# Off-by-one attention with soft expert mixing: two wide products for the negated maxima, and weight pieces fetched in halves

## The chip, the cores and the metric

The kernel runs on one core of a Trainium2 chip. The metric is the device time of one execution in microseconds (us). The core's engines are TensorE (PE, with its weight loads shown apart as PEld), VectorE (DVE), ScalarE (ACT), GpSimd (POOL) and SyncE (SP); DMA transfers are issued from queues of SP and POOL.

## What is computed

Attention over 8 batches and 12 heads, with 448 positions of 64 elements; its softmax has an extra term in the denominator. The result, as 3584 rows of 768, goes through a soft mixture of 8 experts with 4 slots each.

```python
# attention
scores = scale * np.matmul(q, k.transpose(0, 1, 3, 2))
m = np.max(scores, axis=-1, keepdims=True)
e = np.exp(scores - m)
attn = e / (np.sum(e, axis=-1, keepdims=True) + np.exp(-m) + 1e-09)
x = np.matmul(attn, v)            # then laid out as [3584, 768]
# mixture
logits = x @ phi                  # [3584, 32]
d = softmax of logits over the rows; slot_input = d.T @ x
slot_out = relu(slot_input[e] @ w1[e]) @ w2[e]      # for each expert e
out = (softmax of logits over the slots) @ slot_out
```

## The kernel before

**Units and steps.** The attention is done in 24 units (`U`). A unit is two batches (index `b`) times two heads (index `h`): unit `u` is batch pair `u // 6` and head pair `u % 6`. A unit has 7 steps (`TB = 7`), each for 64 of the 448 positions.

A step of the main loop (lines 751 to 761) issues, in this order:

- `stage_S(u, s)`: scores of 128 query rows against all keys. For steps 0 to 5 these are two products with 64 rows and 128 columns of the array, one for each head (L242); for step 6 they are four products of 64 by 64 (L246). VectorE takes the row maxima of the result (L250).
- work planned as "av" and "value": `stage_AV` (L322), the product of the exponentials and the values of an earlier unit, 12 products of 64 by 128 and then 4 of 64 by 64 for each of the 7 position blocks; in step 5 also the transposes of a finished unit (`stage_X`, L402) and of the next unit's q and k (`stage_T`, L227); in step 0 `stage_MT` of the unit before.
- `stage_ST`, ten steps behind `stage_S` (`LAG = 10`): the scores again, transposed, with the negated maxima added, into one PSUM slot, and ScalarE's exponential of them (L295).
- work planned as "end" and "load": parts of the mixture, and DMA issues.

**The negated maxima.** `stage_MT` transposes the maxima of a unit with four products (L258) into `mt`, a tile of 128 partitions and 64 columns. Each partition holds one row of maxima, for a certain head, batch and position block. GpSimd multiplies `mt` by `nmask`, which is -1 where a partition belongs to a position block and batch and 0 elsewhere, and so spreads it over `md`: 128 partitions by two batches by 448 columns (L268 for the 768 columns of the first six position blocks of both batches, L274 for the 128 of the last block). In `stage_ST` four products with a stationary tile of ones, one for each batch and head (L286), sum the 64 partitions of a head, which gives every output partition the negated maximum of its column. Four more products (L291) add the scores. All eight are 64 by 64 pieces of the array, and all have 448 columns.

**PSUM.** `slot` hands out tiles from a ring of three. A step takes one slot for `stage_S` and one for `stage_ST`; transposes and mixture parts take slots of the same ring.

**Weights.** The experts' weights are fetched in 32 pieces of 128 partitions by 3072 elements (768 KB in the source). 24 of them are resident (`wres`). `load_w` (L156 to L169) issues one DMA on POOL's queue for a piece. The plan (L734) issues one whole piece in step 5 of units 2 to 22, and a second one in units 9, 13 and 16. There it stands behind `load_qk`, which issues the four loads of q and k for the unit after the next and waits until the transposes have read the buffer that it fills.

**What sets the order.** It is written out by hand: `at(n, where, f)` puts a piece of work into step `n`, and each engine runs its instructions in the order in which the loop issues them. `stage_ST` for step `n` follows the "av" and "value" work of the step on TensorE.

**Buffers.** Most tiles lie in one large tile `block` whose parts are listed in L73 to L77 (`md0`, `md1` for the spread maxima, with pads that keep other parts at their places).

Of the kernel before, what the change touches and what calls it, by code (L numbers as in the profile page):

```python
# [9 lines left out]
F32 = mybir.dt.float32  # L10
BF16 = mybir.dt.bfloat16
AX = mybir.AxisListType
AF = mybir.ActivationFunctionType
ALU = mybir.AluOpType
PSUM = bass.MemoryType.PSUM

P = 64
# [3 lines left out]
WRES = 24  # L21
# [3 lines left out]
def kernel(  # L25
# [10 lines left out]
    nc = tc.nc  # L36

    B, H, S, D = q.shape
# [5 lines left out]
    TB = S // P  # L44
# [4 lines left out]
    U = BP * HP  # L49
    C3 = TB // 2  # L50
    N2 = 2 * S
# [4 lines left out]
    gdma = nc.gpsimd.dma_start  # L56

    const = ctx.enter_context(tc.tile_pool(name="const", bufs=1))
    small = ctx.enter_context(tc.tile_pool(name="small", bufs=2))
# [8 lines left out]
    def part(name, n, bufs=1):  # L68
        nonlocal size
        parts[name] = size, n, bufs  # L70
        size += n * bufs

    for name, n in (("vr", 2 * N2), ("qk0", 2 * N2), ("qr", N2), ("kr", N2), ("x0", N2),  # L73
                    ("qk1", 2 * N2), ("md0", N2), ("pad0", 256),
                    ("v65", 2 * TB * 66), ("xu", 4 * TB * 65), ("pad1", 328),
                    ("qk2", 2 * N2), ("md1", N2), ("v66", 2 * TB * 66)):
        part(name, n)  # L77
    part("et", N2, 4)
    part("x", N2, HP)
# [10 lines left out]
    def buf(name, i):  # L90
        o, n, bufs = parts[name]
        return block[:, ds(o + (i % bufs) * n, n)]
# [19 lines left out]
    def room(i):  # L112

        return wres[:, i, :] if i < WRES else block[:, ds(rooms[i - WRES], HW)]

    def slot(shape, dtype=F32):
        return ring.tile(shape, dtype, tag="r", name="ps")
# [11 lines left out]
    def load_qk(u):  # L129

        for src, name in ((q, "qr"), (k, "kr")):
            RAW[u, name] = load(u, buf(name, 0).rearrange("p (h n) -> p h n", h=2), src, nc.gpsimd)
# [13 lines left out]
    def load_v(u):  # L146
        t_ = block[:, ds(parts["vr" if u < U - 1 else "qr"][0], 2 * N2)].bitcast(F32).rearrange("p (h n) -> p h n", h=2)
        RAW[u, "vr"] = load(u, t_, v, nc.sync if u else nc.gpsimd)
# [4 lines left out]
    weights = [(kind, 4 * g + e, half) for kind in (1, 2) for g in range(G)  # L153
               for half in range(2) for e in range(4)]

    def load_w(i):  # L156


        kind, e, half = weights[i]
        if kind == 1:  # L160
            J, n = KC // 2, F
            src = moe_w1[e].rearrange("(p j) f -> p j f", p=128)[:, ds(half * J, J), :]
        else:
            J, n = FK // 2, DD
            src = moe_w2[e, ds(half * 128 * J, 128 * J)].rearrange("(p j) f -> p j f", p=128)
        t_ = room(i).rearrange("p (j n) -> p j n", n=n)
        gdma(out=t_, in_=src)  # L167
        for j in range(J):
            W[kind, e, half * J + j] = t_[:, j, :]  # L169

# [3 lines left out]
    ident32 = const.tile([128, 128], F32, name="ident32")  # L174
# [2 lines left out]
    nc.vector.tensor_copy(ident, ident32)  # L177
    first_cast()
    load_qk(1)
    ones = const.tile([128, P], BF16, name="ones")  # L180
    nc.vector.memset(ones, 1.0)

    nmask = const.tile([128, TB, 2], BF16, name="nmask")
    nc.vector.memset(nmask, 0.0)
    for base in (0, -P):
        nc.gpsimd.affine_select(
            out=nmask, in_=nmask, compare_op=ALU.not_equal, fill=-1.0,
            base=base, pattern=[[-1, TB], [-32, 2]], channel_multiplier=1)
    load_v(0)
    M = [const.tile([128, 160], BF16, name=f"m{i}") for i in range(2)]  # L190
    for i in range(2):
# [27 lines left out]
    QT, KT, MD, ET, EM, AV, XU, X, DEN = {}, {}, {}, {}, {}, {}, {}, {}, {}  # L219

    def stage_T(u, name):

        ps = slot([128, 2, S], BF16)
        r = RAW.pop((u, name))
        for t in range(TB):
            for h in range(2):
                nc.tensor.transpose(ps[ds(h * D, D), :, ds(t * P, P)],  # L227
                                    r[:, h, ds(t * D, D)], ident)
        t_ = buf(f"qk{u % 3}", 0)[:, ts(int(name == "kr"), N2)].rearrange("p (b n) -> p b n", b=2)
        nc.vector.tensor_copy(t_, ps)  # L230
        (QT if name == "qr" else KT)[u] = t_

    def maxima(u):
        return M[u % 2][:, ds(32, 128)].rearrange("p (h r) -> p h r", h=2)
# [17 lines left out]
    def stage_MT(u):  # L252

        own = u == 0 or u == U - 1
        ps = slot([128, 2, 32]) if own else AV[u - 1][:, :, ds((2 * C3 + 1) * 65, 32)]
        for half in range(2):
            for a in range(2):
                nc.tensor.matmul(ps[:, a, :], M[u % 2][:, ds(32 - 32 * half, 128)],  # L258
                                 ident[:, ds(half * P + a * 32, 32)], start=(own and half + a == 0),
                                 stop=(half == 1), skip_group_check=True)  # L260
        mt = small.tile([128, P], BF16, tag="mt", name="mt", bufs=1)
        (nc.scalar.copy if u < U - 1 else nc.vector.tensor_copy)(  # L262
            mt.rearrange("p (a n) -> p a n", a=2), ps)
        em = small.tile([128, 2, TB], F32, tag="em", name="em", bufs=3)
        nc.scalar.activation(em, maxima(u)[:, :, ds(0, TB)], AF.Exp, scale=-scale)
        EM[u] = em
        md = buf(f"md{u % 2}", 0).rearrange("p (b n) -> p b n", b=2)
        nc.gpsimd.tensor_tensor(  # L268
            md[:, :, ds(0, C3 * 128)].rearrange("p b (e n) -> p b e n", n=P),
            mt.unsqueeze(1).unsqueeze(1).broadcast_to([128, 2, 2 * C3, P]),  # L270
            nmask[:, ds(0, 2 * C3), :].rearrange("p (b c) a -> p b (c a)", b=2).unsqueeze(3)
                 .broadcast_to([128, 2, 2 * C3, P]),
            op=ALU.mult)
        nc.gpsimd.tensor_tensor(  # L274
            md[:, :, ds(C3 * 128, P)], mt.unsqueeze(1).broadcast_to([128, 2, P]),
            nmask[:, 2 * C3, :].unsqueeze(2).broadcast_to([128, 2, P]), op=ALU.mult)
        MD[u] = md
        if u < U - 1:
            nc.gpsimd.tensor_scalar(em, em, 1e-9, None, op0=ALU.add)

    def stage_ST(u, t):
        ps = slot([128, 2, 512])
        for b in range(2):
            for h in range(2):
                hs = ds(h * D, D)
                nc.tensor.matmul(ps[ds(b * P, P), h, ds(0, S)], ones[hs, :], MD[u][hs, b, :],  # L286
                                 start=True, stop=False)
        for b in range(2):
            for h in range(2):
                hs = ds(h * D, D)  # L290
                nc.tensor.matmul(ps[ds(b * P, P), h, ds(0, S)],  # L291
                                 KT[u][hs, b, ds(t * P, P)], QT[u][hs, b, :],
                                 start=False, stop=True)
        et = buf("et", u * TB + t).rearrange("p (h n) -> p h n", h=2)
        nc.scalar.activation(et, ps[:, :, ds(0, S)], AF.Exp, scale=scale)  # L295
        ET[u, t] = et
# [118 lines left out]
    def mixture(bp, n, at):  # L415
# [119 lines left out]
        if final:  # L535
# [13 lines left out]
            at(n + 5, "small", slot_sum)  # L549
            at(n + 7, "end", slot_in)  # L550
            at(n + 7, "end", lambda: [load_w(WRES + i) for i in (6, 7)])
            at(n + 7, "end", experts_in)
            at(n + 7, "end", experts_hidden)
# [149 lines left out]
    def at(n, where, f):  # L703
        plan.setdefault((n, where), []).append(f)

    for u in range(U):
        n = u * TB
# [23 lines left out]
    for bp in range(BP):  # L731
        mixture(bp, (bp * HP + HP - 1) * TB + 27, at)

    for i, u in enumerate(sorted((*range(2, U - 1), 9, 13, 16))):  # L734
        at(u * TB + 5, "load", lambda i=i: load_w(i))
    at(4, "load", late_constants)
    stage_T(0, "qr")
    stage_T(0, "kr")

    end = TB * U  # L740
    for n, i in ((end - 5, 0), (end - 1, 1), (end + 3, 2), (end + 7, 3), (end + 12, 4),
                 (end + 12, 5)):
        at(n, "load", lambda i=i: load_w(WRES + i))
# [7 lines left out]
    for n in range(last + 1):  # L751
        run(n, "small")
        if n < TB * U:
            stage_S(*divmod(n, TB))
            run(n, "av")
            run(n, "value")
        if 0 <= n - LAG < TB * U:
            stage_ST(*divmod(n - LAG, TB))
        run(n, "value")
        run(n, "end")  # L760
        run(n, "load")
# [56 lines left out]
    for i in range(2, BP * TB):  # L818
# [4 lines left out]
        c, a = divmod(t, 2)  # L823
        cs = ds(32 * c, 32)
        ps = slot([128, 2, 512])
        for half in range(2):
            if i < FT:
                nc.tensor.matmul(ps[:, half, ds(0, 384)], wide[:, ts(i, 128)], so[:, half, :],
                                 start=True, stop=True)
            else:  # L830
                nc.tensor.matmul(ps[:, half, ds(0, 384)], cT[cs, bp, ts(a, 128)], sr[cs, half, :],  # L831
                                 start=True, stop=True, tile_position=(32 * c, 0))
# [34 lines left out]
```

## Time and profile before

| what | value |
|---|---|
| time, median of 3 runs (lowest to highest) | 328.78 us (325.86 to 331.56) |
| the profiled execution: time, and span of its trace | 328.26 us, 326.5 us |
| TensorE clock granted, mean over the span | 0.953 |
| weight pieces kept in `wres` | 24 issues, 768 KB each, 9.3 us to landing (median) |
| loads of q and k, issued from POOL | 46 and 46 issues, 112 KB each, 4.5 and 5.0 us to landing |
| GpSimd's idle time before the q loads, until L227 has read the buffer | 32.0 us |
| GpSimd's second product of the maxima (L274) | 24 times, 399 ns each |
| VectorE's row maxima (L250) | 168 times, 1088 ns each |
| ScalarE's exponentials (L295) | 168 times, 917 ns each |

How to read it: busy times of an engine are the union of its instructions, so two products that run side by side count once. Products are pipelined, and their ends are modelled: a product of 448 columns is shown with some 360 ns, of which its columns take only a part, so the start of the next product says more than the end of the last. "Issue" is time in which an engine waited for nothing that the profile shows. Operations are named by line and by the tiles that they write and read; an operation that the program puts into `block` is shown under that name.

### The profile page before, as it was taken

What the parts mean: (1) busy time and instruction counts of PE and PEld (TensorE: products, weight loads), DVE (VectorE), ACT (ScalarE), POOL (GpSimd) and SP (SyncE); (2) the same over time, 40 slices, a digit from 0 to 9 for tenths busy, and PEclk for the clock granted to TensorE, in tenths of its full rate; (3) what the DMA queues carried; (4) which work ended last, traced back from release to release, by engine and by line L of the source; (5) the groups of instructions that cost most, each with busy time, mean ns of one, the idle gap of its engine ahead of it and who ended that gap; (6) DMA issues with size and microseconds to landing.
All of it is one profiled execution on the core that took longest, in us unless ns stands there. A gap on an engine that the chain in (4) does not pass through costs nothing.

```text
span 326.5 us, 13241 instructions
## 1 busy us (share of the span) xinstructions
PE 281.1 (86%) x5866; PEld 159.0 (49%) x5866; DVE 253.5 (78%) x354; ACT 211.5 (65%) x341; POOL 207.3 (64%) x308
## 2 busy tenths in 40 slices
PE   0669999999999999998999998989999897977910
PEld 0325565555655556554555555555555453532300
DVE  1897999999989989998899888888998547216820
ACT  3015878878778677786787876867877873215610
POOL 5365678898877887888849866969695653300000
PEclk9999999999999999999999999999999999997555
DMA  7346599999998899999998999988799599947997
GB/s 137 66 60 112 102 175 180 178 176 175 179 186 158 131 210 211 194 178 180 216 189 129 165 228 208 153 154 171 167 134 199 103 189 214 214 95 272 398 400 284
DMA packets 30313, 59.33 MB, mean 182 GB/s; under 512 B 4048, under 2 KB 22736, under 8 KB 30256
## 3 DMA queue, kind: packets, MB, share of 16 engines
q0 software_dynamic: 19056, 36.46, 65.2%
q1 hardware_dynamic: 11200, 22.02, 21.0%
q8 instruction: 46, 0.75, 0.9%
q14 instruction: 11, 0.09, 0.1%
HBM read 83.46 MB, written 11.01 MB: 289 GB/s over the span
## 4 chain that ended last, share of the span: by engine, by line
PE 55%; DVE 19%; POOL 6%; DMA 6%; issue 5%; ACT 4%; SPq 0%; POOLq 0%; ACTq 0%; DVEq 0%
PE av L322 13%; DVE m L250 11%; PE ps L242 9%; PE ps L286 9%; PE ps L291 7%; PE ps L227 5%; DMA block<-in_moe_w_dram 4%; PE ps L831 4%; ACT block L295 3%; PE ps L402 3%; DVE block L230 3%; POOL block L268 2%; PE ps L246 2%; DMA wres<-in_q_dram 2%; POOL block L125 1%
## 5 line engine op out<-in xcount | busy, mean ns | idle before, releaser
L250 DVE TENSOR_REDUCE m<-ps 128x2 bf16<-128x896 f32 x168 | 179.7, 1088 | 21.1 <-PE ps L242 17.1
L295 ACT ACTIVATE block<-ps 128x896 bf16<-128x896 f32 x168 | 153.8, 917 | 56.8 <-PE ps L291 51.7
L322 PE MATMUL av<-block 64*128 64x65 bf16 (+1 forms) x2688 | 89.7, 194 | 2.0 <-issue 0.9
L322 PEld LDWEIGHTS <-block 64*128 64x128 bf16 (+1 forms) x2688 | 75.6, 97 | 31.3 <-issue 10.4
L286 PE MATMUL ps<-block,ones 64*64 64x448 bf16 x672 | 69.4, 370 | 6.6 <-POOL block L274 2.9
L291 PE MATMUL ps<-block 64*64 64x448 bf16 x672 | 65.7, 355 | 0.5 <-issue 0.5
L242 PE MATMUL ps<-block 64*128 64x448 bf16 x288 | 54.3, 373 | 4.4 <-DVE m L250 1.8
L125 POOL DMA_DIRECT2D block<-in_q_dram x46 | 29.5, 644 | 32.2 <-PE ps L227 32.0
L242 PEld LDWEIGHTS <-block 64*128 64x128 bf16 x288 | 18.7, 94 | 53.6 <-issue 48.8
L268 POOL TENSOR_TENSOR block<-mt,nmask 128x768 bf16<-128x768 bf16 x24 | 35.8, 1493 | 7.8 <-ACT mt L262 6.5
L350 POOL TENSOR_TENSOR block<-block,rec 128x896 bf16<-128x896 f32 x22 | 37.1, 1688 | 1.5
L286 PEld LDWEIGHTS <-ones 64*64 64x64 bf16 x672 | 24.4, 105 | 11.6 <-issue 6.9
L230 DVE COPY block<-ps 128x896 bf16<-128x896 bf16 x48 | 27.7, 614 | 1.4 <-PE ps L227 1.2
L125 POOL DMA_DIRECT2D block<-in_k_dram x46 | 27.9, 627 | 0.0
L227 PE MATMUL ps<-ident,block 128*64 128x128 bf16 x644 | 24.8, 229 | 1.2 <-issue 0.8
L291 PEld LDWEIGHTS <-block 64*64 64x64 bf16 x672 | 23.8, 107 | 1.0 <-issue 1.0
L300 POOL CAST block<-block 128x896 bf16<-128x896 f32 x24 | 22.3, 931 | 3.1 <-PE ps L291 2.2
L227 PEld LDWEIGHTS <-block 128*64 128x64 bf16 x644 | 20.5, 115 | 4.6 <-issue 2.4
L333 ACT COPY block<-av 128x780 f32<-128x780 f32 x22 | 17.7, 804 | 0.0
L167 POOL DMA_DIRECT2D wres<-in_moe_w_dram x24 | 14.6, 617 | 1.8 <-issue 1.8
L835 DVE COPY wres<-ps 128x768 f32<-128x768 f32 x13 | 12.4, 957 | 3.7 <-PE ps L831 3.4
L403 DVE COPY block<-ps 128x896 bf16<-128x896 bf16 (+1 forms) x23 | 14.0, 607 | 0.7 <-PE ps L402 0.6
(146 smaller groups left out, 243.8 us busy)
## 6 DMA issues: line engine op xcount, KB each, us to landing
wres<-in_moe_w_dram POOLq DMA_DIRECT2D x24, 768.0 KB, 9.3
out_dram<-wres SPq DMA_DIRECT2D x28, 384.0 KB, 4.7
block<-in_v_dram SPq DMA_DIRECT2D x46, 224.0 KB, 4.7
block<-in_moe_w_dram POOLq DMA_DIRECT2D x8, 768.0 KB, 9.7
block<-in_q_dram POOLq DMA_DIRECT2D x46, 112.0 KB, 4.5
block<-in_k_dram POOLq DMA_DIRECT2D x46, 112.0 KB, 5.0
wres<-in_q_dram SPq DMA_DIRECT2D x2, 224.0 KB, 4.5
block<-in_v_dram POOLq DMA_DIRECT2D x2, 224.0 KB, 3.5
```

Of the source, the lines that this page charges most:

```text
L125: eng.dma_start(out=t_[ds(b * P, P), :, :], in_=src[bp * 2 + b, ds(hp * 2, 2)].rearrange("h (p t) d -> p h (t d)", t=TB))
L227: nc.tensor.transpose(ps[ds(h * D, D), :, ds(t * P, P)], r[:, h, ds(t * D, D)], ident)
L230: nc.vector.tensor_copy(t_, ps)
L242: nc.tensor.matmul(ps[:, h, ds(0, S)], QT[u][hs, b, ds(c * 128, 128)], KT[u][hs, b, :], start=True, stop=True)
L250: nc.vector.tensor_reduce(m[:, :, s], ps[:, :, ds(0, S)], axis=AX.X, op=ALU.max)
L268: nc.gpsimd.tensor_tensor(md[:, :, ds(0, C3 * 128)].rearrange("p b (e n) -> p b e n", n=P), mt.unsqueeze(1).unsqueeze(1).broadcast_to([128 ...
L286: nc.tensor.matmul(ps[ds(b * P, P), h, ds(0, S)], ones[hs, :], MD[u][hs, b, :], start=True, stop=False)
L291: nc.tensor.matmul(ps[ds(b * P, P), h, ds(0, S)], KT[u][hs, b, ds(t * P, P)], QT[u][hs, b, :], start=False, stop=True)
L295: nc.scalar.activation(et, ps[:, :, ds(0, S)], AF.Exp, scale=scale)
L300: nc.gpsimd.tensor_copy(t_[:, :, :, ds(0, D)], RAW.pop((u, "vr")).rearrange("p h (t d) -> p h t d", t=TB))
L322: nc.tensor.matmul(o, et[bs, h, ds(c * 128, w)], V65[u][bs, h, t, ds(0, 65)], start=(t == 0 and h == 0 and c == 0), stop=(t == TB - 1), sk ...
L350: (nc.gpsimd if u < U - 2 else nc.vector).tensor_tensor(x.rearrange("p s (h d) -> p h s d", h=2), xv[:, :, :, ds(0, D)], rec.unsqueeze(3). ...
```

## The change

Three things change together.

- The spread maxima `md` now hold 448 columns instead of two times 448. GpSimd multiplies `mt` by `which`, a table that is 1 where a partition belongs to a position block, in one operation. The batch is told apart by the stationary tile: `minus`, 64 partitions by 128 columns for a head, is -1 where a partition's batch is that of the output column. In `stage_ST` two products of 64 by 128, one for each head, take the place of the four with ones. The four products of the scores stay.
- The tables are no longer made with two memsets and two GpSimd selections at the start, but with five VectorE operations from the identity (`masks`), issued in step 5 of unit 0, ahead of its scores.
- `load_w` can fetch a part of the partitions. The 24 resident pieces are fetched in 48 halves of 64 partitions: one in steps 1 and 3 of units 1 to 22 each, two in steps 3 and 4 of unit 0, and one each in step 4 of units 3 and 6. The eight pieces that are fetched at the end stay whole.

```diff
-                    ("qk1", 2 * N2), ("md0", N2), ("pad0", 256),
+                    ("qk1", 2 * N2), ("md0", S), ("pad0", 256 + S),
                     ("v65", 2 * TB * 66), ("xu", 4 * TB * 65), ("pad1", 328),
-                    ("qk2", 2 * N2), ("md1", N2), ("v66", 2 * TB * 66)):
+                    ("qk2", 2 * N2), ("md1", S), ("pad2", S), ("v66", 2 * TB * 66)):
...
-    def load_w(i):
+    def load_w(i, p0=0, rows=128):
...
-        gdma(out=t_, in_=src)
+        gdma(out=t_[ds(p0, rows)], in_=src[ds(p0, rows)])
...
-    ones = const.tile([128, P], BF16, name="ones")
-    nc.vector.memset(ones, 1.0)
-
-    nmask = const.tile([128, TB, 2], BF16, name="nmask")
-    nc.vector.memset(nmask, 0.0)
-    for base in (0, -P):
-        nc.gpsimd.affine_select(
-            out=nmask, in_=nmask, compare_op=ALU.not_equal, fill=-1.0,
-            base=base, pattern=[[-1, TB], [-32, 2]], channel_multiplier=1)
+    which = const.tile([128, TB, 1], BF16, name="which")
+    minus = const.tile([128, 2, P], BF16, name="minus")
+    bsel = const.tile([128, 2, 2], F32, name="bsel")
+
+    def masks():
+
+        rows = ident32.rearrange("p (k x) -> p k x", x=32)
+        main = rows[:, :, ds(0, 2 * C3)].rearrange("p (h a) (b c) -> p c a h b", h=2, b=2)
+        nc.vector.tensor_reduce(which[:, ds(0, 2 * C3), 0].rearrange("p (c a) -> p c a", a=2), main,
+                                axis=AX.XY, op=ALU.max)
+        nc.vector.tensor_reduce(which[:, 2 * C3, :], rows[:, :, 2 * C3], axis=AX.X, op=ALU.max)
+        nc.vector.tensor_reduce(bsel[:, 0, :], rows[:, :, ds(0, 2 * C3)].rearrange("p k (b c) -> p b k c", b=2),
+                                axis=AX.XY, op=ALU.max, negate=True)
+        nc.vector.tensor_reduce(bsel[:, 1, :], rows[:, :, 2 * C3].rearrange("p (h a) -> p a h", h=2),
+                                axis=AX.X, op=ALU.max, negate=True)
+        nc.vector.tensor_tensor(minus, bsel[:, 0, :].unsqueeze(2).broadcast_to([128, 2, P]),
+                                bsel[:, 1, :].unsqueeze(2).broadcast_to([128, 2, P]), op=ALU.add)
...
-        md = buf(f"md{u % 2}", 0).rearrange("p (b n) -> p b n", b=2)
+        md = buf(f"md{u % 2}", 0)
         nc.gpsimd.tensor_tensor(
-            md[:, :, ds(0, C3 * 128)].rearrange("p b (e n) -> p b e n", n=P),
-            mt.unsqueeze(1).unsqueeze(1).broadcast_to([128, 2, 2 * C3, P]),
-            nmask[:, ds(0, 2 * C3), :].rearrange("p (b c) a -> p b (c a)", b=2).unsqueeze(3)
-                 .broadcast_to([128, 2, 2 * C3, P]),
-            op=ALU.mult)
-        nc.gpsimd.tensor_tensor(
-            md[:, :, ds(C3 * 128, P)], mt.unsqueeze(1).broadcast_to([128, 2, P]),
-            nmask[:, 2 * C3, :].unsqueeze(2).broadcast_to([128, 2, P]), op=ALU.mult)
+            md.rearrange("p (e n) -> p e n", n=P), mt.unsqueeze(1).broadcast_to([128, TB, P]),
+            which.broadcast_to([128, TB, P]), op=ALU.mult)
...
     def stage_ST(u, t):
         ps = slot([128, 2, 512])
-        for b in range(2):
-            for h in range(2):
-                hs = ds(h * D, D)
-                nc.tensor.matmul(ps[ds(b * P, P), h, ds(0, S)], ones[hs, :], MD[u][hs, b, :],
-                                 start=True, stop=False)
+        for h in range(2):
+            hs = ds(h * D, D)
+            nc.tensor.matmul(ps[:, h, ds(0, S)], minus[hs].rearrange("p b n -> p (b n)"), MD[u][hs, :],
+                             start=True, stop=False)
...
-    for i, u in enumerate(sorted((*range(2, U - 1), 9, 13, 16))):
-        at(u * TB + 5, "load", lambda i=i: load_w(i))
+    halves = sorted((3, 4, 3 * TB + 4, 6 * TB + 4, *(u * TB + s for u in range(1, U - 1) for s in (1, 3))))
+    assert len(halves) == 2 * WRES
+    for i, n in enumerate(halves):
+        at(n, "load", lambda i=i: load_w(i // 2, i % 2 * P, P))
     at(4, "load", late_constants)
+    at(5, "small", masks)
```

## The prediction

> **What bounds the kernel now.** I read the page's busy line and the shares of the chain that ended last, then busy time by stretches of one unit each, then the groups by line, then a stretch of TensorE's timeline. First the page:
>
> ```profile
> PE 281.1 (86%) x5866; PEld 159.0 (49%) x5866; DVE 253.5 (78%) x354; ACT 211.5 (65%) x341; POOL 207.3 (64%) x308
> ...
> PE 55%; DVE 19%; POOL 6%; DMA 6%; issue 5%; ACT 4%; SPq 0%; POOLq 0%; ACTq 0%; DVEq 0%
> ```
>
> TensorE carries 55% of the chain. Three units in the middle (each from one X transpose, L402, to the next; columns: length, then busy time of PE, PEld, DVE, ACT, POOL):
>
> ```profile
> 44.79:54.42 9.63, 9.59 (x226) 5.68 (x225) 9.10 (x12) 7.64 (x12) 7.97 (x12) 1.00 0.96 178
> 54.42:64.41 9.99, 9.88 (x233) 5.83 (x233) 9.22 (x12) 8.15 (x14) 7.96 (x11) 1.00 0.96 183
> 64.41:73.75 9.34, 9.30 (x225) 5.58 (x226) 8.99 (x12) 7.52 (x12) 7.78 (x11) 1.00 0.94 172
> ```
>
> TensorE is busy for all but 0.04 to 0.11 us of a unit of 9.3 to 10.0; VectorE is next with 9.0 to 9.2. So time added to TensorE in a unit lengthens it, and time taken from GpSimd (8 of 9.6) does not shorten it. The groups that the change touches:
>
> ```profile
> L286 PE MATMUL ps<-block,ones 64*64 64x448 bf16 x672 | 69.4, 370 | 6.6 <-POOL block L274 2.9
> L291 PE MATMUL ps<-block 64*64 64x448 bf16 x672 | 65.7, 355 | 0.5 <-issue 0.5
> L242 PE MATMUL ps<-block 64*128 64x448 bf16 x288 | 54.3, 373 | 4.4 <-DVE m L250 1.8
> L242 PEld LDWEIGHTS <-block 64*128 64x128 bf16 x288 | 18.7, 94 | 53.6 <-issue 48.8
> L268 POOL TENSOR_TENSOR block<-mt,nmask 128x768 bf16<-128x768 bf16 x24 | 35.8, 1493 | 7.8 <-ACT mt L262 6.5
> ```
>
> The first has four products a step, in 64*64 pieces of the array; the third has two a step, in 64*128 pieces, which is the shape that the change gives to the first. Their busy times a step hardly differ: 69.4/168 = 0.41 us for four, 54.3/144 = 0.38 for two. The fourth line is the clue: L242's weight loads stand idle 48.8 us with no releaser. The timeline shows when (start, length, what):
>
> ```profile
> 57.88 0.36 PE L242 MATMUL ps<-block 64*128 64x448 bf16 x2
> 58.07 0.54 PE L322 MATMUL av<-block 64*128 64x65 bf16 x16
> 58.54 0.27 PE L258 MATMUL av<-ident,m 128*128 128x32 bf16 x4
> 58.74 0.38 PE L286 MATMUL ps<-block,ones 64*64 64x448 bf16 x4
> 58.95 0.36 PE L291 MATMUL ps<-block 64*64 64x448 bf16 x4
> 59.24 0.36 PE L242 MATMUL ps<-block 64*128 64x448 bf16 x2
> 59.44 0.49 PE L322 MATMUL av<-block 64*128 64x65 bf16 x14
> 59.73 0.38 PE L286 MATMUL ps<-block,ones 64*64 64x448 bf16 x2
> 59.77 0.20 PE L322 MATMUL av<-block 64*64 64x65 bf16 x2
> 59.80 0.35 PE L286 MATMUL ps<-block,ones 64*64 64x448 bf16 x2
> 59.95 0.40 PE L291 MATMUL ps<-block 64*64 64x448 bf16 x4
> 60.33 0.36 PE L242 MATMUL ps<-block 64*128 64x448 bf16 x2
> ```
>
> From start to start: two products of L242 hold the array 0.19 to 0.20 us; four of L286 hold it 0.21. The pieces work side by side, so two wide products are no cheaper than four narrow ones. But L291's four hold it 0.29 and 0.38 before L242 begins, with the same 448 columns: going from 64*64 to 64*128 pieces costs about 0.1 us more (the rest of the 0.38 is a wait for a PSUM slot). At 59.73 the opposite: L286 starts while narrow products of L322 are still to come, since the shape is the same.
>
> I measured this from the starts of single products between 20 and 250 us, less the time that their columns take (0.187 us for 448): 149 changes from wide to narrow inside L322 cost a median of 93 ns, 117 from L291 to L242 99 ns, and those to and from the 128-row products of L258, L402 and L227 94 to 107. It is a price for each change of shape, paid by nothing else in the stream.
>
> The Trainium skill (TensorEngine Tiling (Array Packing), Key Properties) says that changing the tiling mode, not just the tile, drains TensorE. The trace agrees, with 93 to 99 ns; the page gives no price.
>
> **The change part by part.** *Two products instead of four.* Stream time: 0.21 against 0.19 to 0.20 us, nothing that counts. Changes of shape: an ordinary step (1, 2, 3, 4 and 6 of a unit) runs S, L322 wide, L322 narrow, L286, L291, and now changes twice; with a wide pair between narrow L322 and narrow L291 it changes four times. In steps 0 and 5, L258 or L227 stands before L286, so one change is added. With the overlap: from the first narrow product of L322 to the first of L291 takes 0.23 to 0.26 us now. After, it is 0.053 (the second narrow pair waits for its weights, as in the trace) + 0.027 + 0.095 + 0.187 + 0.095 = 0.46. So 0.215 a step x 5, and 0.095 x 2: 1.27 us a unit. 22 units run so: 27.9 us. The last two have 20 more such changes, 1.9 us among stalls, of which I take 1.0. As a check, the order of the two programs has 500 changes before and 784 after: 284 x 0.095 = 27.0. Bounds of the price: 0 (all of it beside other work) and 0.2 us (L291 to L242 at its worst), which doubles the sum.
>
> *What of it is absorbed.* TensorE now waits for others too. By the list of waits between 100 and 265 us it stands about 9.5 us: 3.2 on nothing shown (four places of 0.5 to 1.0), 1.9 on GpSimd's maxima (L274), the rest on VectorE and L300. Single starts, less 95 ns for each change, give 14 us from 40 to 265. Behind a slower TensorE the others have 1 us more in each unit, so waits on them shrink. Ends 0 and 14; I take 7, the middle, since bursts longer than a unit's slack (the mixture's VectorE work every sixth unit) remain.
>
> *The negated maxima on GpSimd.* L268 (1493 ns) and L274 (399) become one operation of 448 elements; the line through the two rows gives 0.95. GpSimd gets 0.95 us a unit; only the places where TensorE waited for L274 can pay: 1.1 at 21 us, and those in the 14.
>
> *Weight pieces in halves.* 24 issues of 617 ns become 48 of 64 partitions. An issue of half the rows isn't in the trace: between 0.3 and 0.65 us (L125, 64 partitions, 627 to 644); I take 0.6, so +0.6 us a unit, less than the 0.95 saved. They leave POOL's queue at steps 1 and 3, ahead of the unit's q and k loads, which wait for L227 anyway (32 us of idle time), and ahead of L350 and L300: 0.6 us later each, and TensorE waited for L300 0.8 us in all. The three doubled units (9, 13, 16) lose their second piece, and unit 0, where DMA is at 0.5, takes one. That can remove some of the 3.2 us: counted in the 7. SP's queue, with the v loads, keeps its order.
>
> *Start.* Five small VectorE operations go into step 5 of unit 0, where VectorE is the chain (reductions back to back, 10.65 to 16.73 us). Nearest rows: 231 ns (L348) to 420 (L518); at 0.23 they make 1.2 us. The two memsets that go stood where VectorE was idle. Against it the first maxima are ready 0.95 us sooner, and there the chain runs through L268 and L274. Sum 0.2; ends -1 and +1.5. GpSimd's product of the maxima in unit 0 now waits for a VectorE table too, made two steps before it is due, so the unit's other GpSimd work behind it isn't held.
>
> *Sum.* The profiled run took 328.26 us (span 326.46, 1.8 outside it), 0.2% under the median of 328.78. 328.3 + 27.9 + 1.0 - 7 + 0.2 = 350.4; I say 350. With nothing absorbed 357, with 14 absorbed 343.
>
> **The rivals.** *Faster, because products are what costs.* If each product has a price of its own, 336 fewer pay; the 25 to 30 ns between L322's products would make 336 x 0.025 = 8.4 us, and 320. It decides where the changes of shape cost nothing, as when weights are loaded ahead under the narrow products. For it: L322's wide weights are hidden. Against: only within one shape, and L286's four products start within 50 ns of each other. Chance 0.06. The same page of the Trainium skill (Performance Considerations, Instruction Overhead) states some 60 cycles for each matmul, which speaks for this rival; the starts 3 ns apart speak against it.
>
> *Half price.* One of the two added changes is free, because narrow L322 ends long before the pair's PSUM slot is released: 14 + 0.2 - 7, so 335.5. Against: TensorE shows no wait for that slot in the three units above. Chance 0.12, of which 0.08 lies within 2%.
>
> *GpSimd's issues.* At 215.4 us it stood 1.84 us before a weight issue for no reason shown, and TensorE lost 1.1 behind it. If 24 more issues meet that as often (1 of 24), +2 us; if one unit in three does, +10: 360. Chance 0.05.
>
> **How the numbers follow.** Forecast 0.77, whose own range is 343 to 357; rivals 0.06, 0.12, 0.05. The range 338 to 358 leaves out the first rival, most of the second (0.08), and the last. A measurement here tells about 2% from no change, 322.2 to 335.4 us. Faster 0.06, within 0.09, slower 0.85.
>
> **What would show it.** Right: the new pair starts about 0.1 us after the last narrow L322 product's columns, and the first score product about 0.28 us after the pair; units 10.4 to 10.9 us long; VectorE at 0.85 of a unit. The idle time before weight loads, without a releaser, rises at the new line. Wrong: units still 9.6 long, or the pair starting within 30 ns of narrow L322.

## The result, and the profile after

The changed kernel takes 338.28 us (median of 6 runs, 337.40 to 339.58); the kernel before took 328.08 (6 runs, 325.86 to 331.56). The ratio is 1.033, with a 95% interval of 1.028 to 1.038: slower, as forecast, but by 10 us instead of 22. Some executions of a kernel come out 1.5% or more above its fastest; the ratios and their intervals in this document leave these out, the medians do not. In the profiled execution the span grew from 326.5 to 336.6 us. From the page of after:

```profile
PE 302.4 (90%) x5529; PEld 169.7 (50%) x5530; DVE 258.1 (77%) x357; ACT 211.2 (63%) x341; POOL 196.8 (58%) x306
...
PE 76%; DVE 10%; DMA 5%; issue 2%; ACT 1%; POOL 0%; SPq 0%; DVEq 0%; POOLq 0%; ACTq 0%
...
L293 PE MATMUL ps<-block 64*64 64x448 bf16 x672 | 65.0, 377 | 0.0
L288 PE MATMUL ps<-block,minus 64*128 64x448 bf16 x336 | 61.8, 363 | 2.2 <-DVE block L239 0.8
...
L293 PEld LDWEIGHTS <-block 64*64 64x64 bf16 x672 | 19.1, 103 | 34.3 <-issue 34.3
L277 POOL TENSOR_TENSOR block<-mt,which 128x448 bf16<-128x448 bf16 x24 | 22.5, 937 | 16.2 <-ACT mt L271 15.5
L251 PEld LDWEIGHTS <-block 64*128 64x128 bf16 x288 | 14.2, 94 | 32.6 <-issue 31.9
L167 POOL DMA_DIRECT2D wres<-in_moe_w_dram x48 | 28.3, 591 | 1.2
```

TensorE issues 336 products fewer and is busy 21 us longer. Its share of the chain rises from 55% to 76%; GpSimd's falls from 6% to nothing. The weight loads of the four score products of `stage_ST` (L293, the old L291) now stand idle 34.3 us with no releaser, where it was 1.0: a change of shape lies ahead of them. Three units by stretches (length, then busy time of PE, PEld, DVE, ACT, POOL), and a stretch of the timeline (start, length, what):

```profile
46.59:57.12 10.53, 10.53 (x212) 6.18 (x211) 9.37 (x12) 7.64 (x12) 7.53 (x11) 1.00 1.05 199
57.12:68.32 11.20, 10.91 (x219) 6.29 (x217) 9.36 (x12) 7.96 (x14) 7.53 (x11) 1.00 0.89 162
68.32:78.85 10.53, 10.53 (x211) 6.19 (x210) 9.37 (x12) 7.64 (x12) 8.04 (x12) 1.00 0.94 164
```

```profile
61.15 0.36 PE L288 MATMUL ps<-block,minus 64*128 64x448 bf16 x2
61.45 0.38 PE L293 MATMUL ps<-block 64*64 64x448 bf16 x4
61.76 0.36 PE L251 MATMUL ps<-block 64*128 64x448 bf16 x2
61.96 0.52 PE L324 MATMUL av<-block 64*128 64x65 bf16 x16
62.42 0.36 PE L288 MATMUL ps<-block,minus 64*128 64x448 bf16 x2
62.71 0.38 PE L293 MATMUL ps<-block 64*64 64x448 bf16 x4
63.03 0.36 PE L251 MATMUL ps<-block 64*128 64x448 bf16 x2
```

The pair (L288) now holds the array 0.29 to 0.30 us before the first product of L293, and a plain step is 1.26 us from L293 to L293, each time. From single starts, less the time of the columns: 101 changes from narrow L324 to the pair have a median of 99 ns, 144 from the pair to L293 one of 103 ns. All TensorE waits that the list shows between 40 and 240 us fell from 7.9 to 1.1 us.

### The profile page after: what moved, and what is told of

The parts are those of the page before. It is cut to its first block, busy times and chain, and to the rows that moved or that the text cites. A ratio compares the mean times of both kernels' runs of the same rounds, so it can differ in the third digit from the quotient of the medians.

```text
span 336.6 us, 12611 instructions
## 1 busy us (share of the span) xinstructions
PE 302.4 (90%) x5529; PEld 169.7 (50%) x5530; DVE 258.1 (77%) x357; ACT 211.2 (63%) x341; POOL 196.8 (58%) x306
## 4 chain that ended last, share of the span: by engine, by line
PE 76%; DVE 10%; DMA 5%; issue 2%; ACT 1%; POOL 0%; SPq 0%; DVEq 0%; POOLq 0%; ACTq 0%
PE av L324 18%; PE ps L293 15%; PE ps L288 15%; PE ps L251 12%; PE ps L236 5%; DVE m L259 5%; DMA block<-in_moe_w_dram 4%; PE ps L836 3%; PE ps L404 2%; DVE block L239 2%; PE ps L255 2%; DMA wres<-in_q_dram 1%; PE av L267 1%; PE ps L436 1%; DVE block L405 1%
## 5 line engine op out<-in xcount | busy, mean ns | idle before, releaser
L259 DVE TENSOR_REDUCE m<-ps 128x2 bf16<-128x896 f32 x168 | 183.1, 1095 | 31.3 <-PE ps L251 28.5
L324 PE MATMUL av<-block 64*128 64x65 bf16 (+1 forms) x2688 | 87.9, 194 | 0.1
L324 PEld LDWEIGHTS <-block 64*128 64x128 bf16 (+1 forms) x2688 | 73.4, 97 | 28.5 <-issue 6.3
L293 PE MATMUL ps<-block 64*64 64x448 bf16 x672 | 65.0, 377 | 0.0
L288 PE MATMUL ps<-block,minus 64*128 64x448 bf16 x336 | 61.8, 363 | 2.2 <-DVE block L239 0.8
L125 POOL DMA_DIRECT2D block<-in_q_dram x46 | 27.8, 607 | 45.3 <-PE ps L236 40.5
L293 PEld LDWEIGHTS <-block 64*64 64x64 bf16 x672 | 19.1, 103 | 34.3 <-issue 34.3
L277 POOL TENSOR_TENSOR block<-mt,which 128x448 bf16<-128x448 bf16 x24 | 22.5, 937 | 16.2 <-ACT mt L271 15.5
L251 PEld LDWEIGHTS <-block 64*128 64x128 bf16 x288 | 14.2, 94 | 32.6 <-issue 31.9
L167 POOL DMA_DIRECT2D wres<-in_moe_w_dram x48 | 28.3, 591 | 1.2
L288 PEld LDWEIGHTS <-minus 64*128 64x128 bf16 x336 | 17.1, 93 | 11.7 <-issue 2.6
L404 PE MATMUL ps<-ident,block 128*128 128x128 bf16 x168 | 13.8, 221 | 0.5 <-DVE block L382 0.4
```

The lines of the kernel that those rows point to most:

```text
L125: eng.dma_start(out=t_[ds(b * P, P), :, :], in_=src[bp * 2 + b, ds(hp * 2, 2)].rearrange("h (p t) d -> p h (t d)", t=TB))
L167: gdma(out=t_[ds(p0, rows)], in_=src[ds(p0, rows)])
L251: nc.tensor.matmul(ps[:, h, ds(0, S)], QT[u][hs, b, ds(c * 128, 128)], KT[u][hs, b, :], start=True, stop=True)
L259: nc.vector.tensor_reduce(m[:, :, s], ps[:, :, ds(0, S)], axis=AX.X, op=ALU.max)
L277: nc.gpsimd.tensor_tensor(md.rearrange("p (e n) -> p e n", n=P), mt.unsqueeze(1).broadcast_to([128, TB, P]), which.broadcast_to([128, TB, ...
L288: nc.tensor.matmul(ps[:, h, ds(0, S)], minus[hs].rearrange("p b n -> p (b n)"), MD[u][hs, :], start=True, stop=False)
```

## The experiments

All ratios are to the kernel before on the same chip, with 95% intervals.

**Products and halves apart.** Two kernels, each with one part of the change. The first is the changed kernel with

```diff
-    halves = sorted((3, 4, 3 * TB + 4, 6 * TB + 4, *(u * TB + s for u in range(1, U - 1) for s in (1, 3))))
-    for i, n in enumerate(halves):
-        at(n, "load", lambda i=i: load_w(i // 2, i % 2 * P, P))
+    for i, u in enumerate(sorted((*range(2, U - 1), 9, 13, 16))):
+        at(u * TB + 5, "load", lambda i=i: load_w(i))
```

and the second is the kernel before with the opposite edit and the two arguments of `load_w`.

> The changed kernel with whole weight pieces at their old places (step 5 of units 2 to 22, two in units 9, 13 and 16). Theory A (the added changes of shape cost TensorE 1.1 to 1.2 us a unit, and the waits of TensorE for others, some 14 us, vanish behind that): 337 to 341 us, little above the changed kernel; units 4 to 9 at 10.5 to 11.2. Theory B (the products cost the full 22 to 28 us, and the halves gave 10 to 12 back): 348 to 352.

> The kernel before with the resident pieces in halves as in the change, the products as before. Theory A: the halves can only remove waits that the kernel before has, 0 to 5 us of 328: 323 to 328. Theory B (the halves gave 10 to 12 back): 316 to 318. If 24 more issues on GpSimd's queue hurt: 329 to 332.

The products alone took 338.23 us (1.027, 1.021 to 1.033), the same as the whole change; the halves alone 329.02 (0.999, 0.995 to 1.003), the same as before. So the slowdown is that of the products, and the halves neither gave nor took anything that can be measured. The waits of TensorE with the halves alone, over the whole span (waiter, releaser: us in all, times, longest):

```profile
PE av L322 <- issue: 4.0, 4, 2.0
PE ps L286 <- POOL block L274: 2.8, 2, 1.6
PE ps L286 <- issue: 2.5, 2, 1.6
```

They are no smaller than before. This trace is of the second longest of its twelve executions (332.34 us), but two traces of a kernel with halves and four narrow products, further down, tell the same: 3.3 and 5.5 us on nothing shown between 40 and 240 us, where before has 3.2. With the products alone, pieces whole and three units doubled, there are none. What made the waits go is the slower TensorE program, not the smoother transfers.

**The change of shape.** Two kernels that keep the small table and the halves, and differ from the changed kernel only in the maxima's products. The first puts the pair between the wide and the narrow products of `stage_AV` in steps 1, 2, 3, 4 and 6:

```diff
+    def between(u, m, part):
+        n = u * TB + m
+        if part == 1 and u < U - 2 and n % TB not in (0, 5):
+            stage_sinks(*divmod(n - LAG, TB))
```

where `stage_sinks` takes the slot and issues the pair, and `stage_ST` then issues the scores alone. The second has four narrow products:

```diff
-        for h in range(2):
-            hs = ds(h * D, D)
-            nc.tensor.matmul(ps[:, h, ds(0, S)], minus[hs].rearrange("p b n -> p (b n)"), MD[u][hs, :],
-                             start=True, stop=False)
+        for b in range(2):
+            for h in range(2):
+                hs = ds(h * D, D)
+                nc.tensor.matmul(ps[ds(b * P, P), h, ds(0, S)], minus[hs, b, :], MD[u][hs, :],
+                                 start=True, stop=False)
```

> The changed kernel with the two wide products of the negated maxima put ahead of the narrow products of L322 in steps 1, 2, 3, 4 and 6 of a unit, behind the wide ones, so that a step changes shape twice instead of four times. If the price is the change of shape: TensorE gets 5 x 0.19 to 0.23 us a unit back, units fall from 10.5 to about 9.5, and 322 to 329 us result, where the other engines bound it again. If the price lies in the wide products themselves: 337 to 339, units at 10.5.

> The changed kernel with four products of 64 by 64 for the negated maxima, from the small md and halves of the table minus; halves of the weight pieces stay. If the price is the change of shape: units 4 to 9 back to 9.4 to 9.9, 321 to 327 us, below the kernel before by what the halves and the shorter GpSimd work (0.95 us a unit) take from its waits. If the price lay elsewhere in the change: 336 to 339.

They took 326.40 us (0.988, 0.983 to 0.994) and 325.51 (0.986, 0.981 to 0.992). The first still has two wide products, with as many columns and weights as the changed kernel: moving them past four short products gives back 12 us. Its timeline:

```profile
58.24 0.36 PE L252 MATMUL ps<-block 64*128 64x448 bf16 x2
58.44 0.34 PE L330 MATMUL av<-block 64*128 64x65 bf16 x12
58.62 0.35 PE L289 MATMUL ps<-block,minus 64*128 64x448 bf16 x2
58.91 0.22 PE L330 MATMUL av<-block 64*64 64x65 bf16 x2
58.92 0.38 PE L299 MATMUL ps<-block 64*64 64x448 bf16 x2
...
59.33 0.36 PE L252 MATMUL ps<-block 64*128 64x448 bf16 x2
```

Three wide groups follow one another, then two narrow ones that overlap (58.91 and 58.92): two changes in the step, which takes 1.09 us instead of 1.26.

**How much of a price is absorbed.** The same amount of work without a change of shape, given to both kernels: the maxima's products issued twice, in all steps or in three of seven.

```diff
-        for b in range(2):
-            for h in range(2):
-                hs = ds(h * D, D)
-                nc.tensor.matmul(ps[ds(b * P, P), h, ds(0, S)], ones[hs, :], MD[u][hs, b, :],
-                                 start=True, stop=False)
+        for again in (True, False):
+            for b in range(2):
+                for h in range(2):
+                    hs = ds(h * D, D)
+                    nc.tensor.matmul(ps[ds(b * P, P), h, ds(0, S)], ones[hs, :], MD[u][hs, b, :],
+                                     start=True, stop=again)
```

The small dose has `for again in ((True, False) if t % 2 else (False,))`; on the changed kernel the loop stands around the pair.

> The kernel before with the four narrow products of the negated maxima issued twice in each step (the first time closed and then overwritten): about 0.187 us of TensorE a step without a change of shape, 168 x 0.187 = 31.4 us. If some 14 us of waits are absorbed first and the rest is paid in full: 328.5 + 31.4 - 14 = 346 (343 to 348). If nothing is absorbed: 360. If added TensorE time costs half of itself whatever its size: 344, which this run alone can't tell from the first.

> The same as the full dose, but only in steps 1, 3 and 5 of a unit's second scores: 72 x 0.187 = 13.5 us on TensorE. If waits are absorbed first: 328 to 333, since the dose is no larger than the waits. If half is paid whatever the size: 335. If nothing is absorbed: 342.

> The changed kernel with its two wide products issued twice in each step: 168 x 0.187 = 31.4 us on a TensorE that has no waits left. If the waits were absorbed by the change: full price, 338.3 + 31.4 = 370 (366 to 372). If half is paid whatever the size: 354. If other work hides it: 338 to 345.

The doses are 31.4 and 13.5 us of products, reckoned from 0.187 us for 448 columns. On the kernel before, the full dose gave 346.67 us (1.059, 1.053 to 1.065) and the small one 333.82 (1.020, 1.011 to 1.029); by these ratios that is 19.2 and 6.5 us more. On the changed kernel the full dose gave 367.07, 28.8 above 338.28; its regular units went from 10.53 to 11.81 us. So work added to the kernel before is paid in part, some 61% of the large dose and 48% of the small, and on the changed kernel nearly in full. The intervals allow 55 to 68% and 26 to 71%, so whether a small dose is paid less than a large one isn't shown. The small dose came out between the two first forecasts. The full dose came out where I had put it, but the reason was not quite that one: it still waits 5.7 us on nothing shown between 40 and 240 us, so those waits did not simply go because there was more to do.

**What the waits were.** The kernel before with one resident piece in place of 24:

```diff
-        return wres[:, i, :] if i < WRES else block[:, ds(rooms[i - WRES], HW)]
+        return wres[:, 20, :] if i < WRES else block[:, ds(rooms[i - WRES], HW)]
...
-        gdma(out=t_, in_=src)
+        if i in (0, *range(WRES, 32)):
+            gdma(out=t_, in_=src)
```

> The kernel before with one resident weight piece fetched in place of 24, and every resident weight read from it: it leaves out 23 of the 24 transfers, so the experts compute with wrong weights; the instructions of TensorE stay. If the waits that the change absorbed (3.2 us on nothing shown, and those behind GpSimd) come from traffic of the weights: 319 to 324 us, TensorE's waits on nothing shown under 1 us between 40 and 240 us. If they come from TensorE's own rate of instructions or from VectorE: 326 to 329, the waits as before.

It leaves out 23 of the 24 transfers, and the experts read one piece for all; TensorE's instructions stay. It took 318.66 us (0.977, 0.971 to 0.982). Its waits of TensorE between 40 and 240 us:

```profile
PE ps L247 <- DVE block L231: 0.8, 3, 0.3
PE ps L287 <- DVE block L231: 0.8, 3, 0.3
PE ps L243 <- DVE m L251: 0.5, 3, 0.2
PE ps L287 <- DVE acc L412: 0.4, 2, 0.2
```

No wait on nothing shown is left, and none on GpSimd. The fetch of the resident weights costs the kernel before some 8 us, and this kernel is what it would be without that. The run takes out GpSimd's 23 issues with the transfers. That their 0.6 us each made the waits on nothing shown is unlikely: four narrow products from the small table take 0.95 us a unit off GpSimd, and still wait 3.3 and 5.5 us on nothing shown. A regular unit takes 9.45 us:

```profile
53.75:63.20 9.45, 9.38 (x225) 5.40 (x221) 8.68 (x11) 7.61 (x14) 7.39 (x10) 1.00 0.55 101
```

```profile
37.90 0.36 PE L292 MATMUL ps<-block 64*64 64x448 bf16 x4
38.19 0.36 PE L243 MATMUL ps<-block 64*128 64x448 bf16 x2
...
38.89 0.40 PE L292 MATMUL ps<-block 64*64 64x448 bf16 x4
39.28 0.36 PE L243 MATMUL ps<-block 64*128 64x448 bf16 x2
...
41.06 0.37 PE L292 MATMUL ps<-block 64*64 64x448 bf16 x4
41.47 0.37 PE L243 MATMUL ps<-block 64*128 64x448 bf16 x2
```

By single starts, it takes 282, 335 and 392 ns here from the last product of L292 to L243, and 305 or 306 in every plain step of after. The 282 are the columns and a change of shape (187 and 95); the rest is a wait for a PSUM slot. ScalarE's exponentials end at 39.23 and 41.42 us, and the two late starts come 0.05 after that. The busy time of TensorE can't show these waits (9.38 of 9.45), since the modelled end of L292 covers them.

**Whether it is the number of instructions.** The changed kernel with six products of one column ahead of the pair:

```diff
+        for _ in range(3):
+            for h in range(2):
+                hs = ds(h * D, D)
+                nc.tensor.matmul(ps[:, h, ds(0, 1)], minus[hs].rearrange("p b n -> p (b n)"), MD[u][hs, ds(0, 1)],
+                                 start=True, stop=True)
```

> The changed kernel with six products of one column ahead of the wide pair in each step, closed and then overwritten: 12 more instructions a step on TensorE (its loads and products rise from 39.5 to some 47 in a microsecond of the middle), and some 6 x 0.027 = 0.16 us of its time, 168 x 0.16 = 27 us: 365. If waits on nothing shown come with the number of instructions per time, beside the traffic of the weights: 3 us or more of them between 40 and 240 us, in a TensorE that is slower than in the changed kernel, and 368 to 375 us. If a slower TensorE alone hides them: under 0.5 us of them, as in the changed kernel, and 360 to 366.

It took 354.01 us (1.083, 1.073 to 1.092). The six products hold the array 0.09 us, which makes 15 of the 15.7 us. I had put it at 0.16, by 0.027 for each; but two of them start 3 ns apart, one in each half of the rows, so they are three pairs:

```profile
61.90 0.23 PE L289 MATMUL ps<-block,minus 64*128 64x1 bf16 x6
61.99 0.35 PE L293 MATMUL ps<-block,minus 64*128 64x448 bf16 x2
```

The waits on nothing shown came to 1.3 us, between the two marks that I had set. The loads and products a microsecond came to 44.2, not to the 47 that I had expected. By loads and products of TensorE in a microsecond, between 40 and 240 us, the runs stand so:

| kernel | loads and products a us | waits on nothing shown, us |
|---|---|---|
| changed kernel, products issued twice | 37.7 | 0 |
| changed kernel; products alone | 39.3; 39.4 | 0.3; 0 |
| pair before the narrow products | 40.8 | 2.3 |
| halves alone | 43.0 | 5.3 |
| four narrow, small table, whole pieces (two runs) | 43.8; 43.9 | 5.1; 5.5 |
| four narrow, small table, halves (two runs) | 44.1; 44.0 | 3.3; 5.5 |
| before | 44.1 | 3.2 |
| changed kernel, six short products more | 44.2 | 1.3 |
| small dose; full dose on before | 44.8; 45.3 | 3.7; 5.7 |
| before, one resident piece | 45.8 | 0 |

One kernel in two runs has 3.3 and 5.5, so differences of 2 us in the last column tell little. Without the traffic there are none, whatever the number; with it there are next to none below 40 and some in each run above.

The traces tell what these waits are for. The DMA queue q8 carries packets of 16 KB of the kind "instruction" (packets, MB, share) in before, in after, and in after with the six short products:

```profile
q8 instruction: 46, 0.75, 0.9%
...
q8 instruction: 43, 0.70, 0.8%
...
q8 instruction: 51, 0.84, 1.0%
```

After has 672 loads and products fewer than before and 3 packets fewer; the six short products add 2016 and 8 packets. So q8 brings TensorE's instructions, some 220 to 250 in a packet. All 59 waits on nothing shown of the fourteen traces, between 40 and 240 us, end 1.2 to 1.8 us after such a packet has come. A packet comes only every 5 to 7 us, so by chance some one wait in nine would fall there; waits with a releaser end anywhere from 0.04 to 7.7 us after one. So these were waits for TensorE's own instructions, which came late. What makes them late beside the weights stays open: a packet takes 1.1 us in before and 1.05 without the resident fetch, and the traces don't show when it was asked for. It stays open too whether the number of instructions or TensorE's pace decides, since the run made to tell these apart fell between its marks.

**A version faster than both?** The four narrow products from the small table, with the halves and with whole pieces. The run of whole pieces stood beside the doses; the other two stood beside each other:

> Four narrow products from the small table, with whole weight pieces at their old places. If the halves do nothing, as when they were tried alone: 324 to 327, the same as with halves (325.5), and the gain is GpSimd's shorter work. If the gain there came from the halves: 328 to 330.

> Four narrow products from the small table with the halves, beside the same with whole pieces on one chip. If the halves help where GpSimd has room: 0.99 or less of the kernel before, and 0.5% or more under the whole pieces. If not: both at 0.985 to 1.0.

> Four narrow products from the small table with whole pieces at their old places. If the halves matter: 0.995 to 1.0 of the kernel before. If not: the same as with the halves, within 0.5%.

Whole pieces first gave 326.50 us (0.998, 0.993 to 1.002). On one chip halves gave 325.82 (1.000, 0.996 to 1.004) and whole pieces 325.21 (0.994, 0.990 to 0.998). With the 0.986 of the earlier run of the halves, that is four ratios from 0.986 to 1.000. The two of the halves, 0.986 and 1.000, are of one kernel on two chips, and their intervals do not meet: an interval holds the spread beside one kernel before, not that between chips. The small table with narrow products is no slower than before and may be half a per cent faster; the halves show no gain there either. A gain of 1% over the kernel before isn't settled.

## Why the prediction was right and wrong

**The mechanism was right.** Each added change of shape cost 99 to 103 ns, close to the 93 to 99 read from the profile of before, and two wide products cost no less stream time than four narrow ones. With the added changes taken out, by moving the pair or by narrow products, the loss was gone. Of the signs that I had named, the pair starts 0.1 us after the last narrow columns, the scores 0.29 after the pair, and regular units take 10.53 and 10.85; VectorE is busy for 0.89 of a regular unit instead of 0.85. One sign did not come as named: the idle time before weight loads did not rise at the pair's new line (L288: 2.6 us with no releaser, where L286 had 6.9), but at the products behind it (L293: 34.3).

The Trainium skill (TensorEngine Tiling (Array Packing), Key Properties) says that a change of mode drains TensorE; the runs agree in that every change costs, 99 to 103 ns for those added. The Trainium skill (TensorEngine Tiling (Array Packing), Performance Considerations, Instruction Overhead) also says that a product of one column has the same latency as one of 60. The trace of the six short products agrees, as far as starts can tell: from pair to pair it is 28 ns (median) for one column and 29 for 65 (L329). That made no price for the change, in which four products side by side became two: the kernel with the pair moved has 336 products fewer than the one with four narrow ones, and took 326.40 us against 325.51.

**The step that failed: "Ends 0 and 14; I take 7, the middle".** From the third transposes of q and k to the last, 21 units, the lengths are 219.6 us before (24.89 to 244.50), 232.2 after (24.28 to 256.50) and 210.9 (24.08 to 234.98) with one resident piece. The sum charged 1.27 x 21 = 26.7 us there, and the units grew by 12.6. So 14.1 were absorbed, twice the term and the upper end that single starts had given; the middle of two ends is no reason. The step before it had misled me: "TensorE is busy for all but 0.04 to 0.11 us of a unit", so that time added to it lengthens the unit. Busy time with modelled ends is no measure of waits shorter than a product's tail. The 14.1 have two parts.

*Waits beside the fetch of the weights.* The kernel before lost 219.6 - 210.9 = 8.7 us to them, and after the change no more than 0.3 us on nothing shown is left. (These are single traces; four others with narrow products and the whole fetch have 219.0 to 220.1 for the 21 units, and the halves alone, in its long execution, 224.9.) A unit near 200 us shows it: the kernel before needed 11.75 us for 190.20 to 201.95, with TensorE busy for 9.98, where the changed one needs 10.53.

```profile
190.20:201.95 11.75, 9.98 (x225) 5.79 (x224) 9.32 (x12) 7.70 (x12) 7.94 (x11) 1.00 1.08 221
```

*Waits for PSUM slots.* The other 5.4 us are 26.7 less the 232.2 - 210.9 = 21.3 by which the changed kernel is longer than the one without the fetch. Step by step, in a regular unit, from single starts of the first product of `stage_S`:

```
step of the unit       0     1     2     3     4     5     6     sum, ns
before, one piece   1356  1087  1041  1152  1043  2609  1164        9452
  wait at its end      0    53     2   113     4    81     0         253
after               1464  1263  1263  1266  1264  2612  1394       10526
difference           108   176   222   114   221     3   230        1074
```

The wait is the time from the last product of L292 to the next scores above 282 ns, the shortest there (above the 227 of after where the next scores are the four of step 6). Difference and wait together make 0.22 to 0.23 us for a plain step, where the sum had 0.215, and 1.33 for the unit, where it had 1.27. So the price was right, but 0.25 of it fell on time that TensorE had waited before: the regular unit pays 1.07. The units with VectorE's work for the mixture pay 0.61 (11.22 to 11.83). I had seen the 0.38 between L291 and L242 and called a part of it a slot wait, and did not follow it.

**The ends.** For what comes after the last transposes the sum had +2.3 (1.0, and the 22nd unit's 1.27); it was 82.0 before and 80.1 after, -1.9. At the start I had +0.2 and got -0.6. Neither is told from the spread: other kernels with four narrow products (and no dose) have 78.4 to 81.4 behind that mark, and reach the first at 23.9 to 24.1, also with the tables of before. So the +2.3 did not show, and where the added changes of the end went stays open. Sizes at the start: the five VectorE operations took 0.64 us, not 1.2, and GpSimd's product of the maxima 937 ns, close to the 950 of the line through the two rows. The three differences (-7.1 by what was absorbed, -4.2 and -0.8 at the ends) make the 12 us between the forecast and the 10.1 by which the span grew. That 338.28 still lies in my range is little merit: it is its lowest edge.

**The other parts.** Half a piece costs GpSimd 591 ns to issue, as the 0.6 taken, and harms nothing that can be measured; so the rival of GpSimd's issues fell. The rival in which the number of products has the price fell too. The rival at half price came near in its number (335.5) for a reason that isn't its own: neither of the two changes was free.

## What to carry to other kernels

On TensorE, count the changes of array shape in the instruction stream before counting products: here four 64 by 64 products cost what two of 64 by 128 do, and each change between shapes some 0.1 us; if a wide product must come in, put it next to other wide ones. When work is added to an engine that looks fully busy, read from single starts how long the same piece of a step takes in its fastest instance: what the others take more is waiting, and it pays first. A run with the suspected traffic left out tells how much of a kernel's time is such waiting, which no share of busy time does.

## What the runs showed of the hardware that I had not expected

Fetching 23 more resident pieces, all of them off the chain, costs the kernel before 2.3% (0.977, 0.971 to 0.982). A part of it are waits for which the profile shows no releaser, 3.2 us between 40 and 240 us, and each of these ends 1.4 to 1.5 us after a packet of TensorE's instructions has come. A kernel slowed by its TensorE program lost them: times of the changed kernel lie within 0.7% of each other (337.40 to 339.58), those of before within 1.7% (325.86 to 331.56). And pairs of products of one column follow each other at 28 ns, no faster than pairs of 65 columns (29 ns).
